# Second channel product of three of four batches by seven products of quarters in place of eight, with new hand-written orders

## The chip, the cores and the metric

The kernel runs on one core of a Trainium2 chip. The metric is the device time of one execution in microseconds (us), from runs of the same program; the median counts. Beside it stands one execution taken by the hardware profiler, whose trace is what the readings below come from.

The engines are named as the profile names them: PE multiplies matrices, PEld is its loading of the stationary operand, DVE, ACT and POOL are the vector, scalar and general engines, SP issues stores and some loads.

## What is computed

Windowed attention with four sink tokens, then one block that mixes tokens and channels, for 4 batches of 768 tokens, 8 heads of 64 (512 channels).

```python
def _attn_ref(q, k, v, n_sink, window):
    ...
    scores = scale * np.matmul(q, k.transpose(0, 1, 3, 2))
    ...
    scores = np.where(is_sink | in_window, scores, -1000000000.0)
    ...
    return np.matmul(a, v).astype(np.float32)

def _moe_ref(x, w_tok1, w_tok2, w_ch1, w_ch2):
    xt = x.transpose(0, 2, 1)
    h = np.maximum(xt @ w_tok1, 0.0) @ w_tok2
    u = x + h.transpose(0, 2, 1)
    h2 = np.maximum(u @ w_ch1, 0.0) @ w_ch2
    return (u + h2).astype(np.float32)
```

`w_tok1` is 768x256, `w_tok2` 256x768, `w_ch1` 512x1536, `w_ch2` 1536x512. The change is in the last product, `relu(u @ w_ch1) @ w_ch2`: 768x1536 by 1536x512 for each batch.

## The kernel before

**Stages.** Attention is done by pairs of heads, 4 pairs to a batch. Transposed scores come from PE, ACT takes the exponential from PSUM into `pT` (L620), DVE cuts the band out with a minimum against a mask (L638; L631 is the same on POOL), PE multiplies by the values, DVE normalises into `x_sb` (L744, L747). Token mixing follows for each half of the channels: `mix_h`, `mix_u` (its addition is L854) and a transposition into `uT`. Then channel mixing in `mix_channels`: `v1` multiplies `uT` by `w_ch1` in 24 units of four matmuls of 384 columns, each evicted with the relu into `v1T` by ACT (L159) or DVE (L161); and the second channel product, which `whole` makes for one tile of 128 tokens as 12 matmuls of 512 columns (four units of three), with one DVE addition of `u` on eviction (L1140) and one store of 256 KB (L1146). In the last batch the sixth tile is cut by `columns` into pieces of 256, 128 and 128 columns, with additions at L1175 and stores at L1180. All matmuls go through the helper `mm` (L146); in that second product `v1T` is the stationary operand, loaded for each matmul, and `w_ch2` moves.

**One buffer.** `v1T` is one tile for all batches. So each eviction into it waits for the last units of the second product of the batch before (`done["out", b - 1]`). PE's own matmuls of the next batch may run ahead into PSUM, which has eight banks, and be held there.

**Seven products.** The code for another way stood in the kernel, unused: `BY_SEVEN` (L64) lists the batches that take it, and was empty. In it a batch's `v1T` counts as quarters A11 to A22 (half of the tokens by half of the features) and `w_ch2` as quarters B11 to B22 (half of the features by half of the channels). `add_up` makes four sums of quarters of `v1T` on DVE or POOL, in two chunks each, `weight_sums` four of `w_ch2` once, `products` the seven products and what is added to the output.

**Order.** Nothing runs in an order found on the chip. `ORDERED` (L47) is the order of PE's units, one letter a stream: t, m, s, o, h, g the first batch's attention and token mixing; a, b, e, f, k those of the later ones (b and a scores and values of the attention, k token mixing); c the units of `v1`, 24 to a batch; x, and in the new version y, those of the second channel product. `LOADED` (L60) is the order of the loads on POOL's queue: v, q, k of a pair, t and c, d the quarters of the token and channel weights (d0 to d3 are `w_ch2`). The work of the other engines is put in between by `Plan`, which gives every operation a cost, a set of operations it waits for and an engine that is free first, and so fixes each engine's queue when the program is built. On the chip, each queue then runs strictly in that order. The costs in the diff are costs for this plan; they add no instruction by themselves.

Of the kernel before, what the change touches and what calls it, by code (L numbers as in the profile page):

```python
# [16 lines left out]
def kernel(  # L17
# [14 lines left out]
    B, H, S, D = q.shape  # L32
    P = 128
    NT = S // P
    DM = H * D
# [6 lines left out]
    HS = S // 2  # L42
# [2 lines left out]


    ORDERED = (  # L47
# [9 lines left out]
    )  # L57
    ORDER = (1, 2, 7, 6, 4, 5, 3)
    NQ = 6
    LOADED = (  # L60
        "v1 t0 v2 q4 v3 t1 k4 q5 c2 k5 c0 c1 k6 v4 q6 k7 v6 c3 v5 d3 q7 d2 d1 q8 q9 d0 k8 v7 q11 v8 k9 k10 v9 q15 "
        "k12 k11 q10 v10 q12 v14 k13 k14 v15 q13 v11 q14 k15 v13 v12"
    )
    BY_SEVEN = ()  # L64
    BY_DMA = 12
    U_BY_DMA = 2
    MASKED_BY_PE = [(p, g) for p in range(NHP) for g in range(NT // 2) if (p, g) != (NHP - 1, 0)]
# [98 lines left out]
    done = {}  # L166
# [802 lines left out]
    def mix_channels(b):  # L969
        units = []  # L970

        def v1(ft, half):
            def run():
                ps_v1 = tiles["ps_v1", b, ft, half] = bank("mx", HS)
                for ct in range(NC):
                    mm(
                        ps_v1.rearrange("f (t p) -> f t p", p=P), w_ch1[:, ct, ts(ft, P)], uT_half(b, ct, half),
                        start=(ct == 0), stop=(ct == NC - 1),
                    )

            def evict(e):
                if ("v1", b) not in tiles:
                    tiles["v1", b] = v1_pool.tile([P, NF, S], BF16, name="v1T")
                relu(e, tiles["v1", b][:, ft, ts(half, HS)], tiles["ps_v1", b, ft, half])

            op = Op(
                {"ACT": 490.0, "DVE": 550.0}, evict,
                done["out", b - 1] if b else [],
            )
            op.urgent = 1  # L990
            done["v1", b, ft, half] = op
            return unit(664, run, done["uT", b, half] + [done["ch1", ft * NW // NF]], {"mx": [[op]]}, [op])

        NH = NF // 2
        KC = NH // 2
        C2 = DM // 2

        def block(i, j, k0, n):
            return tiles["v1", b][:, j * NH + k0:j * NH + k0 + n, ts(i, HS)]

        def add_up(c):

            k0 = c * KC

            def part(n):
                if ("s", b) not in tiles:
                    tiles["s", b] = s_pool.tile([P, 3, NH, HS], BF16, name="v1_sums")
                return tiles["s", b][:, n, k0:k0 + KC]

            def op(name, out, in0, in1, how, deps):  # L1010
                def run(e):
                    in_order({"DVE": nc.vector, "POOL": nc.gpsimd}[e].tensor_tensor(
                        out=out(), in0=in0(), in1=in1(), op=how,
                    ))

                done[name, b, c] = Op({"DVE": 85.0 + 0.53 * KC * HS, "POOL": 150.0 + 2.2 * KC * HS}, run, deps)
                return done[name, b, c]

            a11, a12, a21, a22 = (lambda i=i, j=j: block(i, j, k0, KC) for i in range(2) for j in range(2))
            v = {(i, j): [done["v1", b, j * NH + k0 + n, i] for n in range(KC)] for i in range(2) for j in range(2)}  # L1020
            before = done["out", b - 1] if b else []
            s1 = op("S1", lambda: part(0), a21, a22, ALU.add, v[1, 0] + v[1, 1] + before)
            s3 = op("S3", a21, a11, a21, ALU.subtract, v[0, 0] + [s1])
            s2 = op("S2", lambda: part(1), lambda: part(0), a11, ALU.subtract, v[0, 0] + [s1])
            s4 = op("S4", lambda: part(2), a12, lambda: part(1), ALU.subtract, v[0, 1] + [s2])
            return [s1, s3, s2, s4]
# [164 lines left out]
        for c in range(2):  # L1191
            for half in range(2):
                units += [v1(j * NH + c * KC + n, half) for j in range(2) for n in range(KC)]
            if b in BY_SEVEN:
                units[-1].then += add_up(c)
        if b not in BY_SEVEN:
            last = b == B - 1
# [29 lines left out]
    def queue(key, op):  # L1227
        done[key] = op
        plan.pending.append(op)
# [26 lines left out]
    def weight_sums(c):  # L1256
        h, k = NF // 2, NF // NW
        b11, b12, b21, b22 = (
            w_ch2[:, j * h + c * k:j * h + (c + 1) * k, ts(g, DM // 2)] for j in range(2) for g in range(2)
        )  # L1260
        t1, t2, t3, t4 = (lambda n=n: sums_tile(n)[:, c * k:(c + 1) * k] for n in range(4))
        loaded = [done["ch2", c], done["ch2", 2 + c]]
        for name, out, in0, in1, of in (
            ("T1", t1, b12, lambda: b11, ()), ("T2", t2, b22, t1, ("T1",)),
            ("T3", t3, b22, lambda: b12, ()), ("T4", t4, b21, t2, ("T2",)),
        ):
            def run(e, out=out, in0=in0, in1=in1):
                in_order({"DVE": nc.vector, "POOL": nc.gpsimd}[e].tensor_tensor(
                    out=out(), in0=in0, in1=in1(), op=ALU.subtract,
                ))  # L1270

            queue((name, c), Op({"DVE": 85.0 + 0.53 * k * DM // 2}, run, loaded + [done[n, c] for n in of]))

    def sums_tile(n):
        while len(w_sums) <= n:
            t = raw_pool.tile([P, 2, NT * D], FP32, name="q_f")
            t = t.rearrange("p h x -> p (h x)").bitcast(BF16)
            w_sums.append(t.rearrange("p (k c) -> p k c", c=DM // 2))
        return w_sums[n]

    for c in range(2 if BY_SEVEN else 0):
        weight_sums(c)
# [18 lines left out]
    for word in ORDERED.split():  # L1301
        name, numbers = word[0], word[1:]
# [38 lines left out]
```

## Time and profile before

| | us |
|---|---|
| median of 3 runs | 205.5 |
| lowest and highest of them | 204.61, 205.73 |
| the profiled execution: its own time | 205.19 |
| the profiled execution: its span, first to last instruction | 203.5 |

The granted clock of PE was 1.0 over that execution. A line of a group reads: line of the kernel, engine, operation, output and inputs, shape, count, then busy time in us and the mean of one in ns, then the idle time of the engine just before them with what ended it. A line of the timeline reads: start and length in us, engine, line, operation, and in brackets the idle time before it. Matmuls overlap in the pipeline of PE, so the mean of one is its passage, not the pace; the pace is read from two starts.

### The profile page before, as it was taken

The numbers are of one execution on the slowest core, as the hardware profiler recorded it, in microseconds if no ns is written. First come the engines' busy times: TensorE is split into PE (matmuls) and PEld (weight loads), VectorE is DVE, ScalarE is ACT, GpSimd is POOL, SyncE is SP. The second block draws the span as 40 slices with busy tenths as digits, with TensorE's granted clock in tenths as the row PEclk, the third lists the DMA queues.
The fourth block names the chain that finished last, engine by engine and source line by source line (L and its number), as shares of the span: only waits on it lengthen the run. The fifth ranks groups of instructions, "written<-read, shape, count | busy, mean of one in ns | idle before, by whom it ended". The sixth has DMA issues, their size and how long they took to land.

```text
span 203.5 us, 5060 instructions
## 1 busy us (share of the span) xinstructions
PE 194.3 (95%) x2095; PEld 116.1 (57%) x2117; DVE 104.4 (51%) x237; ACT 111.1 (55%) x196; POOL 73.0 (36%) x108
## 2 busy tenths in 40 slices
PE   6789999999999999999999999999999999999993
PEld 2346886566565665566665454566765454664453
DVE  4787759667566777774557585722221223001221
ACT  4898789878835566677667234464562002773000
POOL 6199985976969800779110100200000000000000
PEclk9999999999999999999999999999999999999999
DMA  6999999999999994999976422210320113100223
GB/s 195 254 279 166 176 191 170 171 184 187 173 155 163 160 138 60 150 163 142 158 77 128 139 82 81 81 52 3 77 53 35 71 54 127 52 3 0 103 103 103
DMA packets 86151, 24.71 MB, mean 121 GB/s; under 512 B 76145, under 2 KB 83185, under 8 KB 86129
## 3 DMA queue, kind: packets, MB, share of 16 engines
q0 software_dynamic: 67232, 11.80, 73.9%
q1 hardware_dynamic: 18896, 12.60, 23.2%
q8 instruction: 16, 0.26, 0.6%
q14 instruction: 7, 0.05, 0.1%
HBM read 26.75 MB, written 6.29 MB: 162 GB/s over the span
## 4 chain that ended last, share of the span: by engine, by line
PE 80%; DMA 11%; POOL 5%; issue 1%; DVE 1%; SPq 0%; POOLq 0%
PE ps L146 77%; DMA w_ch<-in_moe_w_ch_dram 8%; DMA v_sink_f<-in_v_dram 3%; POOL v_aug L139 2%; POOL q_bf L131 1%; PE ps L549 1%; PE ps L149 1%; POOL w_tok L164 1%; PE ps L531 0%; PE ps L519 0%; SPq L225 0%; POOL q_bf L155 0%; POOL w_ch L164 0%; POOL v_sink L155 0%; DVE v_sink_f L221 0%
## 5 line engine op out<-in xcount | busy, mean ns | idle before, releaser
L146 PE MATMUL ps<-uT,w_ch 128*128 128x384 bf16 x384 | 68.0, 326 | 0.0
L146 PE MATMUL ps<-w_ch,v1T 128*128 128x512 bf16 (+2 forms) x293 | 65.7, 362 | 1.8 <-issue 0.6
L159 ACT ACTIVATE v1T<-ps 128x384 bf16<-128x384 f32 x82 | 39.9, 492 | 36.7 <-PE ps L146 34.5
L620 ACT ACTIVATE pT<-ps 128x1024 bf16<-128x1024 f32 (+1 forms) x48 | 44.3, 951 | 14.7 <-PE ps L146 14.5
L146 PEld LDWEIGHTS <-w_ch 128*128 128x128 bf16 x384 | 36.4, 98 | 23.9 <-issue 0.4
L146 PEld LDWEIGHTS <-v1T 128*128 128x128 bf16 x312 | 28.4, 98 | 27.5 <-issue 0.8
L1140 DVE TENSOR_TENSOR o_sb<-ps,u_sb 128x512 f32<-128x512 f32 x23 | 15.8, 686 | 39.9 <-PE ps L146 24.1
L146 PEld LDWEIGHTS <-w_tok 128*128 128x128 bf16 x192 | 18.3, 98 | 5.5
L139 POOL DMA_DIRECT2D v_aug<-in_v_dram x16 | 16.5, 1030 | 12.9 <-issue 7.0
L131 POOL DMA_DIRECT2D q_bf<-in_q_dram x24 | 19.8, 831 | 1.7 <-DMA w_ch<-in_moe_w_ch_dram 1.1
L131 POOL DMA_DIRECT2D k_bf<-in_k_dram x24 | 19.8, 836 | 1.5 <-DMA w_ch<-in_moe_w_ch_dram 1.2
L854 DVE TENSOR_TENSOR u_sb<-ps,x_sb 128x512 bf16<-128x512 f32 x20 | 13.7, 689 | 11.6 <-PE ps L146 8.0
L638 DVE TENSOR_TENSOR pT<-pT,mask_main 128x1024 bf16<-128x1024 bf16 (+1 forms) x23 | 14.3, 624 | 9.3 <-ACT pT L620 9.2
L146 PEld LDWEIGHTS <-pT 128*128 128x128 bf16 x352 | 14.4, 98 | 3.7 <-issue 0.2
L146 PE MATMUL ps<-qT,kT 64*64 64x192 bf16 (+3 forms) x288 | 16.5, 252 | 0.0
L146 PE MATMUL ps<-v_aug,pT 128*128 128x65 bf16 x352 | 15.9, 194 | 0.0
L146 PE MATMUL ps<-h1T,w_tok 128*128 128x256 bf16 x96 | 14.4, 273 | 0.1
L747 DVE TENSOR_TENSOR x_sb<-ps,recip 128x384 bf16<-128x384 f32 x24 | 12.9, 548 | 0.3
L146 PE MATMUL ps<-x_sb,w_tok 128*128 128x256 bf16 x96 | 12.0, 273 | 0.0
L146 PEld LDWEIGHTS <-kT 64*64 64x64 bf16 (+1 forms) x288 | 6.4, 101 | 7.9 <-issue 6.3
L161 DVE TENSOR_SCALAR v1T<-ps 128x384 bf16<-128x384 f32 x14 | 7.6, 552 | 6.1 <-PE ps L146 5.9
L638 DVE TENSOR_TENSOR pT<-pT,mask_first 128x1024 bf16<-128x1024 bf16 x13 | 8.9, 683 | 1.8 <-ACT pT L620 1.8
(69 smaller groups left out, 136.7 us busy)
## 6 DMA issues: line engine op xcount, KB each, us to landing
out_dram<-o_sb SPq DMA_DIRECT2D x23, 256.0 KB, 2.0
v_aug<-in_v_dram POOLq DMA_DIRECT2D x16, 192.0 KB, 6.7
w_ch<-in_moe_w_ch_dram POOLq DMA_DIRECT2D x8, 384.0 KB, 8.5
q_bf<-in_q_dram POOLq DMA_DIRECT2D x24, 96.0 KB, 6.1
k_bf<-in_k_dram POOLq DMA_DIRECT2D x24, 96.0 KB, 5.9
q_f<-in_q_dram SPq DMA_DIRECT2D x4, 384.0 KB, 5.8
k_f<-in_k_dram SPq DMA_DIRECT2D x4, 384.0 KB, 6.2
w_tok<-in_moe_w_tok_dram POOLq DMA_DIRECT2D x2, 384.0 KB, 6.5
```

What stands on the lines that cost most here:

```text
L131: in_order(nc.gpsimd.dma_start(out=out[:, h], in_=rows[:, h]))
L139: in_order(nc.gpsimd.dma_start(out=v_aug.rearrange("p i t d -> p (i t) d")[:, :, 0:D], in_=v[b].rearrange("h s d -> (h s) d")[2 * hp * S:2 ...
L146: in_order(nc.tensor.matmul(*args, skip_group_check=True, **kwargs))
L149: in_order(nc.tensor.transpose(out, in_, ident))
L159: in_order(nc.scalar.activation(out, in_, AF.Relu))
L161: in_order(nc.vector.tensor_scalar_max(out=out, in0=in_, scalar1=0.0))
L164: return in_order(nc.gpsimd.dma_start(out=out, in_=in_))
L620: in_order(nc.scalar.activation(part(tiles["pT", p][:, :, ds(2 * g, 2)]), of_keys(tiles["ps_s", p, g])[:, :, 0:width(g)], AF.Exp, scale=scale,
L638: in_order(nc.vector.tensor_tensor(out=pt, in0=pt, in1=m, op=ALU.min))
L747: in_order(nc.vector.tensor_tensor(out=x_sb[b][:, :, ds((2 * hp + i) * D, D)], in0=tiles["ps_o", p, i][:, :, 0:D], in1=tiles["recip", p, i ...
L854: in_order(nc.vector.tensor_tensor(out=u_part(b, g, s0, n), in0=tiles["ps_u", b, g, s0], in1=x_sb[b][:, s0:s0 + n, c0:c0 + cn], op=ALU.add,))
L1140: in_order(nc.vector.tensor_tensor(out=o_sb.rearrange("p (g c) -> p g c", g=2), in1=u_rows(b, st), in0=tiles["ps_out", b, st].rearrange("p ...
```

## The change

`BY_SEVEN` becomes batches 1 to 3. For these the second channel product is made by seven products of quarters. Batch 0 keeps `whole`; `columns` is no longer used. For each such batch `mix_channels` returns two streams: x, the seven products for token tiles 0 and 1 of each half (n = 2, two units of six matmuls to a product, 14 units), and y, for tile 2 of each half (n = 1, one unit of six, 7 units). Every matmul has 256 columns. `ORDER` gives the order of products: 1, 2, 7, 6, 4, 5, 3. `ORDERED` and `LOADED` are written anew, and three costs of the plan are changed.

The parts of `products` that the prediction follows, unchanged, with the sums they use:

```python
s1 = op("S1", lambda: part(0), a21, a22, ALU.add, v[1, 0] + v[1, 1] + before)
s3 = op("S3", a21, a11, a21, ALU.subtract, v[0, 0] + [s1])
s2 = op("S2", lambda: part(1), lambda: part(0), a11, ALU.subtract, v[0, 0] + [s1])
s4 = op("S4", lambda: part(2), a12, lambda: part(1), ALU.subtract, v[0, 1] + [s2])
...
TERMS = {
    1: ((0, 0), "B11"), 2: ((0, 1), "B21"), 3: ("S4", "B22"), 4: ((1, 1), "T4"),
    5: ("S1", "T1"), 6: ("S2", "T2"), 7: ("S3", "T3"),
}
...
a1 = evict("a1", (0, 0), lambda: u_block(0, 0))
a6 = evict("a6", (1, 0), lambda: u_block(1, 0))
c7 = evict("c7", (1, 1), lambda: u_block(1, 1))
a5 = evict("a5", (1, 1), lambda: sb(1, 1), [c7])
a3 = evict("a3", (0, 1), lambda: u_block(0, 1))
c4 = evict("c4", (1, 0), lambda: sb(1, 0), [a6])
b2 = evict("b2", (0, 0), lambda: sb(0, 0), [a1])
```

Products 1, 6, 5, 3 follow one another in one PSUM bank (a), 7 and 4 in another (c), 2 in a third (b). Each is evicted by one DVE addition, and the next product of its bank adds to what stands there, so it waits until that eviction has read the bank. Two stores leave for each stream: rows of the first half after a3 and b2, rows of the second after a5 and c4.

```diff
--- before.py
+++ after.py
@@ -45,23 +45,24 @@
 
 
     ORDERED = (
-        "t0-1 m0 s0 m1-2 t2 s1 t3 s2 m3 s3 o0 m4 t4 s4 m5 o1 t5 s5 o2 m6 t6 s6 m7 o3 s7 t7 m8 o4 s8-10 m9-10 g0 "
-        "s11 e0 s12 o5-6 g1 o7-8 g2-4 h0-1 g5-7 e1 h2-4 a0 h5-6 a1 e2 a2 h7 c0-6 a3 b0 a4 c7-11 b1 e3 a5 b2 "
-        "c12-13 b3 c14-15 a6 b4 a7 b5-6 c16-18 e4 a8 c19-20 k0 c21 a9 b7 a10 k1 c22 x0 c23 a11 b8 x1 k2 x2 b9-10 "
-        "x3 e5 b11-13 x4-6 e6 a12-13 x7-9 k3 x10 k4 x11-12 k5 b14 a14 f0 x13-14 k6 x15 k7 a15-16 b15-16 x16-17 f1 "
-        "e7 a17 x18-19 b17 x20-22 c24 a18 b18 e8 b19 x23 c25-27 b20 c28 a19-20 b21 c29-32 k8 a21 b22 a22 c33 b23 "
-        "c34-35 b24 c36-38 k9 c39-43 a23 b25 a24 c44-47 b26 k10 x24 b27 a25 b28 a26 x25-26 k11 x27 a27-28 k12 "
-        "x28-32 a29 b29 a30 x33 b30 x34 k13 x35 b31 k14 x36-37 a31-32 b32 x38 b33 x39-40 b34 x41-42 b35 a33-34 "
-        "x43-45 k15 b36 a35 b37-38 c48 x46-47 c49-52 b39 c53 b40 c54 k16 c55-56 b41 c57 x48 k17 c58 k18 c59 "
-        "k19-20 c60-62 k21-22 c63-71 x49-52 c72 x53-58 c73 x59-60 c74 x61-62 c75 k23 x63-71 c76-94 x72 c95 x73-94"
+        "t0-1 m0-1 s0 t2 m2 s1 t3 s2 m3 s3 m4-5 o0 t4 s4 t5 s5 o1-2 m6 t6 s6 o3 m7 t7 s7 m8 o4 s8-10 m9 g0 m10 "
+        "s11-12 g1 o5-8 g2-5 h0-1 g6 e0-1 h2-4 a0 h5-6 g7 h7 e2 a1 c0-4 b0 a2-3 c5-8 a4-5 b1-2 c9-12 b3 e3-4 b4-5 "
+        "c13-17 b6 c18 a6-7 c19-21 x0 c22 a8-9 b7 k0 c23 x1-2 a10 e5 b8-10 x3-4 k1 x5 a11-12 x6-7 a13 b11 k2 x8 "
+        "e6 a14 b12-13 x9-12 a15 b14 a16 k3-4 x13-14 e7 f0 a17 x15 k5 x16-18 k6-7 x19-21 b15 f1 e8 x22 b16 x23 "
+        "c24 b17 c25-27 a18 b18 a19 b19-20 c28-29 b21 a20-21 c30 k8 c31-32 a22 b22 a23 b23 c33-42 k9 b24 k10 "
+        "c43-44 a24-25 b25-27 k11 x24 a26 c45-47 x25 b28 a27-28 x26 y0 k12 a29 b29 x27 y1 b30 x28 k13 y2 x29-30 "
+        "b31 x31 y3 x32 k14 x33 y4 x34-35 a30 b32 a31 b33-34 x36 y5 a32 b35 a33 x37 c48 k15 c49 y6 c50-51 b36 "
+        "a34-35 c52 b37-38 c53 k16 c54 b39 c55 k17 c56-57 b40 k18 b41 c58 x38 k19 c59-61 k20 c62-63 k21 y7 k22 "
+        "c64-65 x39 c66-67 x40 c68 x41 c69-72 y8 c73 k23 x42 c74 x43 y9-10 x44-46 y11 x47-49 y12 c75 x50 c76 x51 "
+        "y13 c77-92 y14 c93-95 y15 x52-58 y16 x59-62 y17 x63 y18-19 x64-65 y20"
     )
     ORDER = (1, 2, 7, 6, 4, 5, 3)
     NQ = 6
     LOADED = (
-        "v1 t0 v2 q4 v3 t1 k4 q5 c2 k5 c0 c1 k6 v4 q6 k7 v6 c3 v5 d3 q7 d2 d1 q8 q9 d0 k8 v7 q11 v8 k9 k10 v9 q15 "
-        "k12 k11 q10 v10 q12 v14 k13 k14 v15 q13 v11 q14 k15 v13 v12"
+        "v1 t0 v3 v2 t1 q4 k4 c2 c0 k5 q5 q6 c1 v4 q7 c3 k6 v5 k7 d3 d2 k8 d0 q9 d1 v6 v8 q8 v7 k12 k9 q13 v11 "
+        "q11 q10 k10 k11 v13 q15 v10 q14 v9 v12 k13 q12 v14 v15 k15 k14"
     )
-    BY_SEVEN = ()
+    BY_SEVEN = range(1, B)
     BY_DMA = 12
     U_BY_DMA = 2
     MASKED_BY_PE = [(p, g) for p in range(NHP) for g in range(NT // 2) if (p, g) != (NHP - 1, 0)]
@@ -1013,7 +1014,7 @@
                         out=out(), in0=in0(), in1=in1(), op=how,
                     ))
 
-                done[name, b, c] = Op({"DVE": 85.0 + 0.53 * KC * HS, "POOL": 150.0 + 2.2 * KC * HS}, run, deps)
+                done[name, b, c] = Op({"DVE": (1012.0 if name == "S3" else 755.0), "POOL": 150.0 + 2.2 * KC * HS}, run, deps)
                 return done[name, b, c]
 
             a11, a12, a21, a22 = (lambda i=i, j=j: block(i, j, k0, KC) for i in range(2) for j in range(2))
@@ -1269,7 +1270,7 @@
                     out=out(), in0=in0, in1=in1(), op=ALU.subtract,
                 ))
 
-            queue((name, c), Op({"DVE": 85.0 + 0.53 * k * DM // 2}, run, loaded + [done[n, c] for n in of]))
+            queue((name, c), Op({"DVE": 150.0 + 0.53 * k * DM // 2}, run, loaded + [done[n, c] for n in of]))
 
     def sums_tile(n):
         while len(w_sums) <= n:
```

## The prediction

> **What bounds the kernel now.** I read the page's shares first, then what PE waited for, then the pace of its matmuls in the timeline.
>
> ```profile
> span 203.5 us, 5060 instructions
> PE 194.3 (95%) x2095; PEld 116.1 (57%) x2117; DVE 104.4 (51%) x237; ACT 111.1 (55%) x196; POOL 73.0 (36%) x108
> ...
> PE 80%; DMA 11%; POOL 5%; issue 1%; DVE 1%; SPq 0%; POOLq 0%
> ```
>
> PE is busy 95% of the span and is 80% of the chain that ended last. The list of PE's waits is short:
>
> ```profile
> PE ps L146 <- DVE ones L173: 1.5, 1, 1.5
> PE ps L531 <- DVE k_bf L155: 1.2, 3, 0.5
> PE ps L146 <- issue: 0.6, 4, 0.2
> PE ps L146 <- DMA w_ch<-in_moe_w_ch_dram: 0.4, 1, 0.4
> ```
>
> All of them but 0.6 us of issue and 0.4 us for a weight's landing lie in the first 16 us. From there PE is the bound, and work taken from PE shortens the end as long as nobody else becomes late. But a busy PE isn't proof of pace, so I read the pace from starts. Twelve matmuls of 256 columns, each with its own stationary operand, in token mixing:
>
> ```profile
> 143.57 1.47 PE L146 MATMUL ps<-x_sb,w_tok 128*128 128x256 bf16 x12
> 144.88 2.11 PE L146 MATMUL ps<-uT,w_ch 128*128 128x384 bf16 x12
> ```
>
> (144.88 - 143.57) / 12 = 0.109 us for one. The second channel product's own pace shows in the tail, where nothing else runs:
>
> ```profile
> 189.92 0.69 DVE L1140 TENSOR_TENSOR o_sb<-ps,u_sb 128x512 f32<-128x512 f32 x1 [1.90 <-PE ps L146]
> 192.51 0.69 DVE L1140 TENSOR_TENSOR o_sb<-ps,u_sb 128x512 f32<-128x512 f32 x1 [1.90 <-PE ps L146]
> ...
> 197.63 0.69 DVE L1140 TENSOR_TENSOR o_sb<-ps,u_sb 128x512 f32<-128x512 f32 x1 [1.90 <-PE ps L146]
> 198.94 0.42 DVE L1175 TENSOR_TENSOR o_sb<-ps,u_sb 128x256 f32<-128x256 f32 x1 [0.62 <-PE ps L146]
> 199.61 0.29 DVE L1175 TENSOR_TENSOR o_sb<-ps,u_sb 128x128 f32<-128x128 f32 x1 [0.24 <-PE ps L146]
> 200.28 0.29 DVE L1175 TENSOR_TENSOR o_sb<-ps,u_sb 128x128 f32<-128x128 f32 x1 [0.38 <-PE ps L146]
> ```
>
> A tile of twelve matmuls of 512 columns takes 192.51 - 189.92 = 2.59 us, 0.216 us each. Twelve of 256 columns take 198.94 - 197.63 = 1.31 us, again 0.109 each, now with v1T as stationary; twelve of 128 take 200.28 - 199.61 = 0.67 us, 0.056 each. So the time goes with the columns, and more loads of the stationary operand don't show:
>
> ```profile
> L146 PEld LDWEIGHTS <-v1T 128*128 128x128 bf16 x312 | 28.4, 98 | 27.5 <-issue 0.8
> ```
>
> a load lasts 98 ns, yet matmuls with a load each follow every 56 ns.
>
> **The change, part by part.**
>
> *Products.* Eight products of quarters are 72 matmuls of 512 columns in a batch: 6 x 2.59 = 15.54 us. The last batch has five such tiles, 12.95, and the pieces, 1.31 + 2 x 0.67: 15.60 us. Seven products are 7 x 18 = 126 matmuls of 256 columns at 0.109: 13.76 us (1.31 / 12 x 126). Gain 1.78 + 1.78 + 1.84 = **5.40 us** of PE time.
>
> The Trainium skill, "TensorE: Matmul & The Clock Gate", section "Back-to-back issue gap", has a rule against this: in a stream of pairs of load and matmul the spacing is set by both, about 81 ns at 128 columns and 131 ns at 512. A straight line between gives an estimate of 98 ns at 256, so 126 would take 12.3 us against 9.4 us for 72, a loss of 2.9 us a batch, and the time would be near 205.2 + 8.7 = 213.9. The trace doesn't agree: 216 ns at 512 and 56 ns at 128. I go by the trace, and keep what it would mean as a rival.
>
> *Sums of v1T.* New on DVE: eight operations of 128x1152 for each batch, 24 in all, both inputs in SBUF. Nearest rows, by shape:
>
> ```profile
> L638 DVE TENSOR_TENSOR pT<-pT,mask_main 128x1024 bf16<-128x1024 bf16 x12 | 8.2, 685 | 2.5 <-ACT pT L620 2.5
> L638 DVE TENSOR_TENSOR pT<-pT,mask_main 128x768 bf16<-128x768 bf16 x11 | 6.1, 557 | 6.8 <-ACT pT L620 6.7
> ```
>
> 128 ns for 256 columns more, so 0.75 us at 1152. The other bound is the pace of an addition from PSUM, 0.69 us at 512 and 0.42 at 256 columns: 0.27 per 256, 1.36 us at 1152. I take 0.75 for three of four; for S3, which overwrites its own input in rows with gaps, 1.0, between the two, since the mask also overwrites its input, without gaps. That's 2 x (3 x 0.75 + 1.0) = 6.5 us a batch (6.0 to 10.9).
>
> *Sums of w_ch2.* Eight operations of 128x768, once: 8 x 0.56 = 4.5 us (to 7.7 at the slower pace, 8 x 0.96).
>
> *Additions to the output.* Seven of 512 and seven of 256 columns take the place of six of 512: 7 x (0.69 + 0.42) - 6 x 0.69 = +3.6 us a batch on DVE.
>
> Together DVE gets 3 x 10.1 + 4.5 = 35 us more, on 104. What hides it is DVE's idle time, and the three stretches differ:
>
> ```profile
> 80.00:133.00 53.00, 52.42 (x579) 30.97 (x584) 34.99 (x74) 30.25 (x49) 16.88 (x29) 1.00 1.02 118
> 133.00:203.50 70.50, 66.98 (x425) 38.76 (x428) 15.09 (x27) 23.06 (x47) 0.00 (x0) 1.00 0.19 60
> 55.00:80.00 25.00, 24.05 (x393) 14.35 (x400) 17.42 (x38) 13.63 (x26) 14.19 (x20) 1.00 1.60 138
> ```
>
> (Columns: stretch, length, then PE, PEld, DVE, ACT, POOL.) Batches 2 and 3 fall after 133 us, where DVE is busy 15 of 70: 20 us more cost nothing there. Batch 1 falls into 80 to 133 with the attention of batches 2 and 3: 35.0 + 6.5 + 3.6 = 45.1 us of DVE work, or 49.6 with all sums of w_ch2, in 53 - 1.8 = 51.2 us. It fits, at 97% in the worst case; and evictions of v1T and copies of q and k that DVE does now can go to ACT, idle 23 us there. I count it as hidden, and price the other case as a rival.
>
> *New waits on PE.* A product on a sum waits for v1T's eviction and the chain S1, S3. Tightest is the last batch: between its last v1 unit (c95) and the second half of product 7 (x57) stand y15 and x52 to x56, 36 matmuls, 3.93 us. The chain: 0.16 until ACT starts, 0.49 for the eviction,
>
> ```profile
> 184.03 0.49 ACT L159 ACTIVATE v1T<-ps 128x384 bf16<-128x384 f32 x1 [0.16 <-PE ps L146]
> ```
>
> 0.75 + 1.0 for the sums, and 0.69 + 0.42 for two output additions queued on DVE between them: 3.5 us, so covered by 0.4. In batch 2 stand c72, y8, c73, k23, x42, c74 between: 3 x 0.65 (0.49 + 0.16 in that row, as ACT keeps step with PE) + 2 x 0.66 + 4 x 0.109 = 3.7 us against a like chain with k23's addition. A product that follows its bank's eviction needs about 0.16 + 0.69 = 0.85 us; the orders put at least two units of y (1.31 us) there at the end. If S3 or DVE's queue is late, product 7 waits, and behind it in PE's queue everything. Bounds: nothing, to one uncovered eviction (0.85) in each of three batches, 2.6. I take **+0.6**, near the low end as the covers exceed the chains.
>
> *The end.* The last addition grows from 128 to 256 columns, +0.13. The last store from 64 to 256 KB:
>
> ```profile
> out_dram<-o_sb SPq DMA_DIRECT2D x23, 256.0 KB, 2.0
> out_dram<-o_sb SPq DMA_DIRECT2D x1, 128.0 KB
> out_dram<-o_sb SPq DMA_DIRECT2D x2, 64.0 KB, 1.6
> ```
>
> +0.4, and up to 0.4 more where the 512 KB of x's last store are still on the way (1.07 us at the slope of these rows, less 0.66 head start). I take **+0.53**.
>
> *Moved steps.* In the first attention the masks m1 and m5 go ahead of other units, and e0 and e1, which turn q4 and k4, behind o8 and h1. In POOL's queue q4 goes from 4th to 6th place, behind v3 and t1, k6 from 13th to 17th, v6 from 17th to 26th, q7 from 21st to 15th, d0 from 26th to 23rd, d1 from 23rd to 25th. Each place is one or two issues:
>
> ```profile
> L131 POOL DMA_DIRECT2D q_bf<-in_q_dram x24 | 19.8, 831 | 1.7 <-DMA w_ch<-in_moe_w_ch_dram 1.1
> L139 POOL DMA_DIRECT2D v_aug<-in_v_dram x16 | 16.5, 1030 | 12.9 <-issue 7.0
> 55.37 0.81 PE L146 MATMUL ps<-w_ch,v1T 128*128 128x512 bf16 x2 [0.38 <-DMA w_ch<-in_moe_w_ch_dram]
> ```
>
> The one load that PE waits for later than 16 us is a w_ch quarter, 0.38 us, and d0 comes earlier. q4 leaves up to two issues (2.1 us) later, but PE asks for it later too. Between -0.4 (that wait goes) and +1.0 (one issue of a load uncovered); I take 0, the nearest row being a wait of 0.38 in the whole trace, of either sign.
>
> *Sum* against the profiled execution: 205.19 - 5.40 + 0.6 + 0.53 = **200.9 us**; that execution stands 0.3 below the median of the runs, and I leave it so. Low 205.19 - 5.40 + 0.53 - 0.4 = 199.9; high 205.19 - 5.40 + 2.6 + 0.93 = 203.3.
>
> **The rivals.**
>
> *The batch boundary eats part.* v1T is one buffer, so c72 to c76 stay in five PSUM banks until x51 and y13 have run, while x and y hold two more for their a and one or two for c. Before, PE ran through that boundary and ACT and DVE emptied the banks after it:
>
> ```profile
> 171.68 1.02 DVE L161 TENSOR_SCALAR v1T<-ps 128x384 bf16<-128x384 f32 x2 [1.90 <-PE ps L146]
> 171.74 1.73 ACT L159 ACTIVATE v1T<-ps 128x384 bf16<-128x384 f32 x4 [17.50 <-PE ps L146]
> ```
>
> With eight banks taken, a unit waits for the last additions, 0.69 + 0.42, and one eviction, 0.49: 1.6 us at each of two boundaries, with 5.40 and 0.53 as above 200.3 + 3.2 = **203.5**. For it: the counts come to seven or eight banks. Against it: b's banks are free long before.
>
> *DVE becomes the bound, slower.* In the stretch of batch 1. If the sums run at the slower pace, it has 35.0 + 10.9 + 7.7 + 3.6 = 57.2 us to do in 51.2: 6.0 over, **206.3**. Or the sums are quick, but DVE's queue is as strictly in order as now and sits idle for the exponentials as it did:
>
> ```profile
> DVE pT L638 <- ACT pT L620: 7.2, 7, 3.2
> ```
>
> 35.0 + 7.2 + 14.6 = 56.8, 5.6 over, 205.9; both together about 213. It decides the sign from 5 us over. Against it: the mask, also two inputs from SBUF, has the quick pace; ACT has room; the sums of w_ch2 can go ahead of 80 us.
>
> *Loads of the stationary operand stick out.* Each of 54 loads more per batch costs its 98 ns: 3 x 5.3 = 15.9, **216**. Only the twelve by twelve of the tail speak to it, and against it.
>
> **How the numbers follow.** My forecast has 0.62, the boundary 0.19, DVE as the bound 0.13 (two thirds of it over 206.5), the loads 0.03; 0.03 stay for anything else. The predicted time is the forecast's, 200.9. From 199.8 to 204.4 lies the forecast's own range and the boundary's case with 0.9 us to spare; left out are the other rivals and a stray. What this measurement can tell from no change is about 0.5%, 1 us. Faster: 0.62 + 0.19 and 0.02 of a part of the DVE case, 0.83. The same, 204.5 to 206.5: 0.06. Slower: 0.11.
>
> **What would show it.** The products of x and y at a pace of 0.109 us, 13.8 us of PE for each batch; sums of 0.75 and 1.0 us; PE's waits on DVE sums and additions at 0.6 us in all; DVE below 95% between 80 and 131 us; about 0.5 us more between the last matmul and the end. Wrong it would be if PE's idle time after 16 us grew by over 2.6 us, or if matmuls of 256 columns kept a longer pace than those of the token mixing.

## The result and the profile after

| | before | changed |
|---|---|---|
| median, us | 205.54 (4 runs, 204.61 to 205.73) | 203.16 (4 runs, 202.71 to 204.03) |
| ratio to before, 95% interval | | 0.9898 (0.9853 to 0.9943) |
| profiled execution: time, span, us | 205.19, 203.5 | 203.24, 201.5 |

Faster by 1.0%, where 2.2% was forecast: the sign is right, the time lies in the range, the size is off by half. Taken again in a later series, the changed kernel gave 203.44 us (ratio 0.9914, 0.988 to 0.9948).

First the page of the changed kernel, its span and shares:

```profile
span 201.5 us, 5425 instructions
PE 193.1 (96%) x2255; PEld 130.6 (65%) x2255; DVE 135.7 (67%) x289; ACT 110.2 (55%) x196; POOL 85.0 (42%) x122
```

DVE rose by 31 us (35 were counted), and PE fell by 1.2 us only; but a busy PE is no pace. The lines of the helper `mm` moved by one, to L147. The pace, in the timeline, inside batch 2's products (start, length, engine, line, operation, count; `q_f` holds the sums of w_ch2):

```profile
162.50 2.13 PE L147 MATMUL ps<-q_f,v1T 128*128 128x256 bf16 x18
164.46 2.13 PE L147 MATMUL ps<-q_f,v_sums 128*128 128x256 bf16 x18
166.43 0.81 PE L147 MATMUL ps<-uT,w_ch 128*128 128x384 bf16 x4
```

18 matmuls in 1.96 and 1.97 us: 0.109 us each, as forecast. What PE waited for:

```profile
PE ps L147 <- DVE v1T L1013: 0.5, 1, 0.5
...
PE ps L550 <- DMA q_bf<-in_q_dram: 0.4, 1, 0.4
```

The two longest of the new ones. The first is in the last batch, at the second half of product 7:

```profile
184.27 2.36 POOL L1013 TENSOR_TENSOR v_sums<-v_sums,v1T 128x1152 bf16<-128x1152 bf16 x1 [48.89 <-DVE v_sums L1013]
184.43 2.81 DVE L1013 TENSOR_TENSOR v1T<-v1T 128x1152 bf16<-128x1152 bf16 x1
185.97 0.82 PE L147 MATMUL ps<-q_f,v1T 128*128 128x256 bf16 x6
187.30 0.83 PE L147 MATMUL ps<-q_f,v1T 128*128 128x256 bf16 x6 [0.51 <-DVE v1T L1013]
```

S3 took 2.81 us on DVE while POOL made S2 beside it. Six matmuls from 185.97 would have been through at 186.63; the next began at 187.30, 0.67 us later. And the end:

```profile
194.58 2.13 PE L147 MATMUL ps<-w_ch,v_sums 128*128 128x256 bf16 x18
196.09 1.08 DVE L1059 TENSOR_TENSOR o_sb<-ps,u_sb 128x512 f32<-128x512 f32 x2 [0.88 <-PE ps L147]
```

PE is done at 194.58 + 18 x 0.109 = 196.54; the second of these additions begins at 196.09 + 1.08 - 0.42 = 196.75. From there to the end of the span it's 4.75 us; before, from 200.28 to 203.5, it was 3.2: the end grew by 1.5 us, to the 0.1 us to which the spans are given. How long stores took from issue to landing, on the page after:

```profile
out_dram<-o_sb SPq DMA_DIRECT2D x12, 256.0 KB, 3.0
out_dram<-o_sb SPq DMA_DIRECT2D x6, 512.0 KB, 2.8
```

So the account of the profiled execution is: products -5.4, the wait on S3 +0.7, the end +1.5, in sum -3.2. The span fell by 2.0. **1.2 us** are left that none of these explains; the wait of 0.4 on q5's load is a first trace of them.

### The profile page after: what moved, and what is told of

Its sections match the earlier page's. It is cut to its first block, busy times and chain, and to the rows that moved or that the text cites. A ratio compares the mean times of both kernels' runs of the same rounds, so it can differ in the third digit from the quotient of the medians.

```text
span 201.5 us, 5425 instructions
## 1 busy us (share of the span) xinstructions
PE 193.1 (96%) x2255; PEld 130.6 (65%) x2255; DVE 135.7 (67%) x289; ACT 110.2 (55%) x196; POOL 85.0 (42%) x122
## 4 chain that ended last, share of the span: by engine, by line
PE 79%; DMA 10%; POOL 3%; DVE 3%; issue 1%; SPq 0%; ACT 0%; POOLq 0%
PE ps L147 77%; DMA w_tok<-in_moe_w_tok_dram 4%; DMA q_bf<-in_q_dram 4%; DMA v_sink_f<-in_v_dram 3%; PE ps L550 2%; POOL v_aug L140 1%; DVE v1T L1013 1%; DVE o_sb L1059 1%; PE ps L520 1%; SPq L226 0%; POOL k_bf L132 0%; POOL w_tok L165 0%; POOL q_bf L132 0%; POOL q_bf L156 0%; POOL v_sink L156 0%
## 5 line engine op out<-in xcount | busy, mean ns | idle before, releaser
L147 PE MATMUL ps<-uT,w_ch 128*128 128x384 bf16 x384 | 68.5, 326 | 0.0
L160 ACT ACTIVATE v1T<-ps 128x384 bf16<-128x384 f32 x80 | 39.1, 492 | 36.5 <-PE ps L147 36.0
L147 PEld LDWEIGHTS <-w_ch 128*128 128x128 bf16 x384 | 36.5, 98 | 22.0 <-issue 0.4
L147 PEld LDWEIGHTS <-v1T 128*128 128x128 bf16 x288 | 27.4, 98 | 10.6 <-DVE v1T L1013 0.8
L147 PE MATMUL ps<-w_ch,v1T 128*128 128x256 bf16 (+1 forms) x180 | 31.5, 315 | 0.0
L1013 POOL TENSOR_TENSOR v_sums<-v_sums,v1T 128x1152 bf16<-128x1152 bf16 x2 | 4.7, 2362 | 49.8 <-DVE v_sums L1013 49.8
L147 PEld LDWEIGHTS <-w_tok 128*128 128x128 bf16 x192 | 18.1, 98 | 4.3 <-issue 0.4
L1059 DVE TENSOR_TENSOR o_sb<-ps,u_sb 128x512 f32<-128x512 f32 (+1 forms) x24 | 12.9, 553 | 9.0 <-PE ps L147 7.8
L147 PEld LDWEIGHTS <-v_sums 128*128 128x128 bf16 x162 | 15.6, 98 | 2.3 <-issue 0.2
L632 POOL TENSOR_SCALAR_AFFINE_SELECT pT<-pT 128x256 bf16<-128x256 bf16 (+1 forms) x20 | 8.6, 463 | 19.3 <-ACT pT L621 16.8
L147 PE MATMUL ps<-qT,kT 64*64 64x192 bf16 (+3 forms) x288 | 16.6, 255 | 0.0
L147 PE MATMUL ps<-v_aug,pT 128*128 128x65 bf16 x352 | 15.3, 194 | 0.2 <-DMA v_aug<-in_v_dram 0.2
L147 PEld LDWEIGHTS <-pT 128*128 128x128 bf16 x352 | 13.8, 97 | 2.3 <-issue 0.4
L147 PE MATMUL ps<-h1T,w_tok 128*128 128x256 bf16 x96 | 14.4, 273 | 0.0
L147 PE MATMUL ps<-q_f,v1T 128*128 128x256 bf16 x108 | 13.8, 273 | 0.5 <-DVE v1T L1013 0.5
L1059 DVE TENSOR_TENSOR o_sb<-ps,o_sb 128x512 f32<-128x512 f32 (+1 forms) x18 | 9.9, 554 | 6.2 <-PE ps L147 6.1
L147 PE MATMUL ps<-q_f,v_sums 128*128 128x256 bf16 x108 | 13.4, 273 | 0.0
```

The lines of the kernel that those rows point to most:

```text
L147: in_order(nc.tensor.matmul(*args, skip_group_check=True, **kwargs))
L160: in_order(nc.scalar.activation(out, in_, AF.Relu))
L632: in_order(nc.gpsimd.affine_select(out=pt, in_=pt, compare_op=ALU.is_ge, fill=0.0, base=-n, pattern=[[0, nk], [1 - 2 * n, P]], channel_mul ...
L1059: in_order(nc.vector.tensor_tensor(out=sb(*out), in0=tiles["ps_out", b, t0, key[0]], in1=in1(), op=ALU.add,))
```

## The experiments

All changes are against the changed kernel, unless said otherwise. Ratios are to the kernel before, measured beside it.

| kernel | median, us | ratio (95% interval) |
|---|---|---|
| again | 203.44 | 0.9914 (0.988 to 0.9948) |
| dve_sums | 202.58 | 0.9879 (0.9839 to 0.9919) |
| tail_cols | 202.00 | 0.9846 (0.9805 to 0.9886) |
| both | 201.37 | 0.9806 (0.9783 to 0.9828) |
| last_eight | 202.38 | 0.9875 (0.9836 to 0.9913) |
| eight_dve | 202.39 | 0.9860 (0.9828 to 0.9891) |
| batch1_eight | 203.51 | 0.9938 (0.9915 to 0.996) |
| batch2_eight | 202.85 | 0.9912 (0.9885 to 0.994) |
| both_again | 201.16 | 0.9827 (0.9798 to 0.9855) |
| all_eight | 206.32 | 1.0077 (1.0047 to 1.0107) |
| both_third | 201.59 | 0.9825 (0.9789 to 0.9862) |
| q5_early | 201.26 | 0.9812 (0.9779 to 0.9846) |
| e2_later | 205.02 | 0.9986 (0.9968 to 1.0003) |
| start_old | 203.24 | 0.9915 (0.9886 to 0.9944) |
| old_head | 207.10 | 1.0111 (1.0076 to 1.0146) |
| new_head | 209.86 | 1.0234 (1.021 to 1.0257) |
| before_again | 205.63 | 1.0018 (1.0001 to 1.0035) |

### The sum on POOL

```diff
-                done[name, b, c] = Op({"DVE": (1012.0 if name == "S3" else 755.0), "POOL": 150.0 + 2.2 * KC * HS}, run, deps)
+                done[name, b, c] = Op({"DVE": 755.0}, run, deps)
```

> All sums of v1T on DVE, none on POOL (two were). Theory 1 (a sum on POOL slows the sum that runs on DVE beside it): S3 of the last batch falls from 2.81 to 0.76 us, PE's wait of 0.51 us before product 7 goes, and the time falls by 0.5 to 0.7 us to about 202.5. Rival (S3 is slow because it overwrites its own input): S3 stays above 1.0 us and the time stays at 203.2.

Measured 0.86 us below the changed kernel beside it, where 0.5 to 0.7 were expected. The edit also lowers S3's cost in the plan; the order of PE's and ACT's work stays the same. In the groups by shape, S3 (v1T<-v1T) of the changed kernel, then of this one:

```profile
L1013 DVE TENSOR_TENSOR v1T<-v1T 128x1152 bf16<-128x1152 bf16 x6 | 8.4, 1407 | 0.1
```

```profile
L1013 DVE TENSOR_TENSOR v1T<-v1T 128x1152 bf16<-128x1152 bf16 x6 | 4.5, 753 | 0.1
L1013 DVE TENSOR_TENSOR v_sums<-v_sums,v1T 128x1152 bf16<-128x1152 bf16 x6 | 4.5, 750 | 0.0
```

In place or not, 0.75 us. In the changed kernel's own trace, too, the four S3 that ran without a sum on POOL took 0.75 to 0.76 us, and the two beside one 2.61 and 2.81. Overwriting its own input costs S3 nothing; the company on POOL did, and PE's wait on S3 is gone.

### The last stores

```diff
+            by_columns = b == B - 1
+            s00, s01, s10, s11 = (store_columns(i, g) for i in range(2) for g in range(2))
+            for st, o in ((s00, b2), (s01, a3), (s10, c4), (s11, a5)):
+                st.deps.append(o)
...
-                3: product(3, "a", a3, a5, [st0]),
+                3: product(3, "a", a3, a5, [s01 if by_columns else st0]),
```

(s00 goes with product 2, s10 with 4, s11 with 5.)

> In the last batch each store is cut in two by columns, the half that is complete early leaves early: behind the last product only 256 KB of x and 128 KB of y are left in place of 512 and 256. Theory 1 (the last store waits behind the 512 KB ahead of it): from its issue to its landing 1.6 to 2.0 us in place of 2.96, the time falls by about 1.0 us to 202.2. Rival (a store's landing has a fixed length, and shorter rows are slower): from issue to landing 2.8 us or more, the time stays within 0.3 us of 203.2 or grows.

Measured 1.4 us below the changed kernel beside it. Its last two additions and the four small stores:

```profile
196.50 1.08 DVE L1059 TENSOR_TENSOR o_sb<-ps,u_sb 128x512 f32<-128x512 f32 x2 [0.89 <-PE ps L147]
```

```profile
out_dram<-o_sb SPq DMA_DIRECT2D x4, 128.0 KB, 2.0
```

```profile
span 200.8 us, 5424 instructions
```

From the last addition's start, 196.50 + 1.08 - 0.42 = 197.16, to the end it's 3.6 us in place of 4.75. So the landing isn't fixed. This edit halves the last store and the one ahead of it alike, and so doesn't tell the two apart. The trace of the changed kernel does; its twelve stores of this kind:

```profile
DMA to landing us min/median/max: 2.0/2.8/3.0
```

The shortest, 2.0 us, is one of 256 KB issued 2.7 us behind the store ahead of it. The last one, also 256 KB, is issued 0.48 us behind the 512 KB and lands 2.96 us after its issue: about 1 us for the bytes ahead.

> Sums of v1T on DVE alone and stores of the last batch by columns, together. If the two costs are separate, the gains add: 203.3 - 0.9 - 1.4 = 201.0 us, no wait on S3 and a landing of the last store within 2.0 us. If one covers the other: 202.0.

Both cures together: 201.37 us, 1.9 under 203.24 (start_old beside it, below, which is as fast as the changed kernel) and 2.1 under 203.44, of 2.3 for the sum. This is faster than either of the two kernels compared.

### What seven products give, batch by batch

The last batch by eight, first with the plan still free to put sums on POOL (last_eight), then with all of them on DVE (eight_dve):

```diff
-    BY_SEVEN = range(1, B)
+    BY_SEVEN = range(1, B - 1)
...
-        ... y13 c77-92 y14 c93-95 y15 x52-58 y16 x59-62 y17 x63 y18-19 x64-65 y20"
+        ... y13 c77-95 x52-74"
```

> Seven products in batches 1 and 2 alone, the last batch by eight as before, with its small last pieces. Theory 1: PE's gain of 1.84 us in the last batch is given back there by the wait on S3 (0.67) and the longer end (1.57), so the time falls by about 0.4 us against the changed kernel, to 202.8. Rival (the gain of the last batch is real and was lost elsewhere, in the start or in batch 1): the time grows by 1.2 us or more, to 204.4 or above.

202.38: taking the change out of the last batch made the kernel faster by 1.06 us, even more than expected. As the change was made, its third batch was a loss.

> Seven products in batches 1 and 2, the last batch by eight, sums on DVE alone. In the last batch seven products save 1.84 us of PE; if the wait on S3 and the long end were all that ate it, the kernel with both cures (201.4) is faster than this one by 1.2 to 1.8 us, so 202.6 to 203.2 here. If something else in the last batch eats the saving too, the two are within 0.4 us.

202.39, 1.0 us over the 201.37 of the kernel with both cures, which was measured on another chip (by the ratios 1.1): a little under the expected range. The rows say where PE stood. Last additions of eight_dve, then of the kernel with both cures:

```profile
197.83 0.29 DVE L1176 TENSOR_TENSOR o_sb<-ps,u_sb 128x128 f32<-128x128 f32 x1 [0.38 <-PE ps L147]
```

```profile
195.38 1.08 DVE L1059 TENSOR_TENSOR o_sb<-ps,u_sb 128x512 f32<-128x512 f32 x2 [0.89 <-PE ps L147]
```

The last addition starts at 197.83 and at 195.38 + 1.08 - 0.42 = 196.04: seven products end 1.79 us earlier (1.84 forecast), and 0.7 of it go to a still longer end.

Then batches 1 and 2, each by eight products in the kernel with both cures:

```diff
-    BY_SEVEN = range(1, B)
+    BY_SEVEN = (2, 3)
```

(or `(1, 3)`; the 21 units of x and y of that batch become 24 units of x in the same places.)

> The kernel of both cures, with batch 1 by eight products: its 21 units of x and y become 24 units of three matmuls of 512 columns in the same places, batches 2 and 3 stay by seven. If batch 1's gain of 1.78 us of PE arrives in full at the end: 201.4 + 1.8 = 203.2. If the 1 us that is still missing is lost in batch 1 (DVE at 9.8 of 10 us between 110 and 120): 202.2 or less.

> The same with batch 2 by eight products, batches 1 and 3 by seven. If batch 2's gain of 1.78 us arrives in full: 203.2. If the missing 1 us is lost at its boundaries: 202.2 or less. If both this and batch 1 give 1.8, the missing 1 us lies ahead of the products, in the first 97 us.

> The kernel of both cures again, beside the other two: 201.4 us, within 0.4.

203.51 and 202.85 against 201.16: by the medians batch 1 costs 2.35 us, batch 2 1.69. Not all of that is the products. Up to a batch's first unit of the second channel product the two kernels make the same units, and still they don't come there together. That unit of batch 1 in batch1_eight and in both_again:

```profile
106.17 0.81 PE L138 MATMUL ps<-w_ch,v1T 128*128 128x512 bf16 x3
105.66 0.82 PE L147 MATMUL ps<-w_ch,v1T 128*128 128x256 bf16 x6
```

and that of batch 2 in batch2_eight and in both_again:

```profile
140.33 0.81 PE L138 MATMUL ps<-w_ch,v1T 128*128 128x512 bf16 x3
140.94 0.82 PE L147 MATMUL ps<-w_ch,v1T 128*128 128x256 bf16 x6
```

The spans are 201.8, 200.4 and 199.4 us. batch1_eight is 0.5 us late before its batch begins and 2.4 at the end: 1.9 us for batch 1. batch2_eight is 0.6 us early and then 1.0 late: 1.6 us for batch 2. For the last batch the spans of eight_dve and of the cured kernel, 200.8 and 199.7, give 1.1 us, where 1.84 less the 0.7 of the longer end were due. So the products yield about what was forecast, in every batch, and what is missing lies outside them.

> The new orders of units and loads, with eight products in all batches: the units of x and y become units of three matmuls of 512 columns in the same places, or next after the last v1 unit of their batch; the end is that of the kernel before, and no sums are made. If the missing 1 us is the new order's, ahead of the products: 206.2 to 206.6, 1 us over the kernel before on the same chip. If the new order costs nothing: within 0.4 us of the kernel before.

> The kernel of both cures beside it: 201.2 to 201.4, and 5.0 us below the new order with eight products (5.4 of PE less 0.45 at the end).

The new orders with no product by seven: 206.32 us, **1.3 us slower than the kernel before** (ratio 1.0077, 1.0047 to 1.0107, which is 1.0 to 2.2 us), and 4.7 us above the cured kernel beside it. There 5.40 were due, less the 0.45 by which the cured end is still longer than that of before (3.82 us from PE's last matmul to the end of the span, against 3.37): 4.95. Its page and what PE waited for:

```profile
span 204.5 us, 5074 instructions
```

```profile
PE ps L541 <- DMA q_bf<-in_q_dram: 0.6, 1, 0.6
PE ps L523 <- DVE k_bf L147: 0.5, 2, 0.3
PE ps L138 <- issue: 0.3, 2, 0.2
```

The missing 1.2 us come with the new orders as a whole, also without a product by seven.

### Where the new orders lose it

> The changed kernel itself, taken again. Theory 1 (the start differs by execution): in the first profile PE ran at half pace until 10.6 us (512 columns in 427 ns) where the kernel before had left it at 6.1 us, with the same matmuls on PE up to there; in another execution the change to full pace comes at another time, and the times spread by about 1 us, 202.7 to 204.0. Rival (the new order of the first attention causes it): again half pace until about 10.6 us, and a spread no wider than 0.3 us.

> The kernel before, taken again for its start. If the time at which PE reaches full pace differs by execution, it may be at 6 or at 10 us here, and the idle time of PE before 20 us changes by 0.3 to 0.8 us with it; if the order fixes it, again 6.1 us.

The start does differ by execution, and in the kernel before as well. Four masks in its first profile and in its second:

```profile
7.11 0.93 PE L146 MATMUL ps<-mask_add,ident 128*128 128x512 bf16 x4
```

```profile
7.65 1.67 PE L146 MATMUL ps<-mask_add,ident 128*128 128x512 bf16 x4
...
9.44 0.38 PE L146 MATMUL ps<-qT,kT 64*128 64x256 bf16 x4
```

The second time PE runs at half pace until 9.3 us. Yet both spans are 203.5 us: the half pace cost nothing that reached the end. The same units of that kernel at 31 us, in the first profile and in the second:

```profile
30.86 0.36 PE L146 MATMUL ps<-qT,kT 64*64 64x192 bf16 x8
```

```profile
31.43 0.36 PE L146 MATMUL ps<-qT,kT 64*64 64x192 bf16 x8
```

The second execution is 0.57 us late there, and at 92.7 us only 0.03 (rows further down). In between, the first waits 0.38 us for a quarter of w_ch at 55.4 us, and the second doesn't. The changed kernel taken again left the half pace at 9.3 to 9.6 us, where its first profile had left it at 10.6; so theory 1 of the start holds, but as an explanation of the missing time it falls, since the slower start of before lost no time.

For the old order of units up to o0:

> The changed kernel with the old order of units up to o0 alone, the first 14 us; the loads stay as changed. If the new order of the start costs 0.5 us: 202.8 and less idle time on PE before 20 us. If not: 203.3, within 0.3.

203.24: nothing. For the old order and loads up to the first unit of v1 in the changed kernel (old_head, shown here), and the new ones in the kernel before (new_head):

```diff
-        "t0-1 m0-1 s0 t2 m2 s1 t3 s2 m3 s3 m4-5 o0 ...
+        "t0-1 m0 s0 m1-2 t2 s1 t3 s2 m3 s3 o0 m4 ...
...
-        "v1 t0 v3 v2 t1 q4 k4 c2 c0 k5 q5 q6 ...
+        "v1 t0 v2 q4 v3 t1 k4 q5 c2 k5 c0 c1 ...
```

> The changed kernel with the old order of units up to the first unit of v1 and the old order of loads. Theory 1: 203.2 us, within 0.4. Rival (the new order of the first attention or of the loads costs 1.2 us): 202.0 or less, full pace on PE from about 6 us.

> The kernel before with eight products, but with the new order of units up to the first unit of v1 and the new order of loads. Theory 1 (the start's extra 1.2 us in the profile isn't the order's): 205.5 us, within 0.4. Rival (the new order of the first attention or of the loads costs it): 206.5 or more, with half pace on PE until about 10 us.

Both mixtures are slower than both kernels, 207.10 and 209.86, and decide nothing: each brought a wait of its own, such as this one in old_head, for a later load,

```profile
PE ps L541 <- DMA q_bf<-in_q_dram: 2.7, 1, 2.7
```

since the rest of the order was made for other landings. They show how much such an order is worth, and that half of one can't be tried alone.

A wait before e2, for q5, shows in most profiles with the new loads, with 0.2 to 1.0 us (both_again and eight_dve don't have it). Two ways to take it away, moving PE's unit, or the load:

```diff
-        ... g7 h7 e2 a1 c0-4 b0 a2-3 ...
+        ... g7 h7 a1 c0-2 e2 c3-4 b0 a2-3 ...
```

> The changed kernel with one unit of PE moved: e2, which turns q5 and k5, goes behind three of the five v1 units that followed it, about 2 us later. Theory (q5's load, moved from 8th to 11th place, lands at 32.1 us and PE stands before e2 for 0.4 to 1.2 us): the wait on that load goes and the time falls by 0.4 to 1.0 us to about 202.7. Rival (the wait only moves, since the scores of that pair are next and late by as much): the time stays at 203.3, and PE waits for the copies of q5 or k5 instead.

The wait is gone, others have come (0.8 us on a load of v, 0.4 on an addition to the output), and the median rose to 205.02. Moving one unit also reordered the work of ACT, DVE and POOL behind it, and the profiled execution was the fastest of twelve (203.65), so what slowed the others isn't known.

```diff
-        "v1 t0 v3 v2 t1 q4 k4 c2 c0 k5 q5 q6 ...
+        "v1 t0 v3 v2 t1 q4 k4 k5 q5 c2 c0 q6 ...
```

> The kernel of the two cures (sums on DVE alone, last stores by columns), with q5 and k5 loaded ahead of the two first quarters of w_ch1 in place of behind them; PE's order stays but for the buffers' names. Theory (PE waits before e2 because q5's load came three places later): the wait of 0.6 us on that load goes, 200.7 us. Rival (the loads bound the first 65 us together, so the wait moves to w_ch1 or a later load): 201.4, with a wait on another load in its place.

201.26, no gain over 201.37. The wait before e2 is gone, and PE waits for a k later:

```profile
44.16 0.35 PE L550 MATMUL ps<-ident,k_bf 64*128 64x64 bf16 x12 [0.48 <-DMA k_bf<-in_k_dram]
```

The rival holds. Where the orders lose can be read at one place. Ahead of b22 in the old order and of a22 in the new one the kernels have made the same units, 1257 matmuls. The row that follows, in the kernel before, in its second profile, in the changed kernel and in all_eight:

```profile
92.71 0.28 PE L146 MATMUL ps<-v_sink,pT_sink 64*128 64x65 bf16 x8
92.74 0.28 PE L146 MATMUL ps<-v_sink,pT_sink 64*128 64x65 bf16 x8
93.68 0.36 PE L147 MATMUL ps<-qT,kT 64*64 64x192 bf16 x8
93.34 0.36 PE L138 MATMUL ps<-qT,kT 64*64 64x192 bf16 x8
```

The changed kernel is 1.0 us late there and all_eight 0.6, ahead of any product by seven. Counted by the loads of the stationary operand, all twelve profiles that keep both new orders up to this place are late against the first one of the kernel before, by 0.2 to 1.8 us and by 1.1 in the mean. On average 0.6 us of it arise between 31 and 37 us, where most of them wait before e2. So most of what is missing is lost in the first 93 us. Which of the moved loads and units cause it stays open, since curing the wait for q5 brought nothing.

## Why the prediction was wrong

**Right: the products.** 5.40 us of PE, at 0.109 us a matmul; by single batches 1.9, 1.6 and 1.1 us arrived, where 1.78, 1.78 and 1.1 were due, and over all_eight 4.7 of 4.95. The rule of the Trainium skill, "TensorE: Matmul & The Clock Gate", section "Back-to-back issue gap" (131 ns at 512 columns, 81 at 128), didn't hold here: the kernel before shows 216 and 56 ns, and 256 columns go at 109 ns in products whose every matmul loads its own stationary operand. The rival of loads that stick out is gone with it.

The forecast for the profiled execution was -5.4 + 0.6 + 0.53 = -4.3 us, and the span fell by 2.0. The missing 2.3 us are two terms of the sum.

**Wrong, the largest step: the moved steps.** They were taken at 0, between -0.4 and +1.0. The new orders alone cost 1.3 us (all_eight), and the changed kernel has lost 1.0 us by 93 us. The step failed twice: the prediction listed q4, k6, v6, q7, d0 and d1 but not q5, which moved from 8th to 11th place and is the load that the changed kernel's PE waits for longest (0.4 us, and 1.0 taken again; a v costs 0.2 and 0.3); and it argued from single loads, where the early loads and units are a chain in which a wait cured in one place comes back in another (q5_early, e2_later).

**Wrong: the end.** The forecast took +0.53 us, from medians of landings (1.6 and 2.0 us), and put at most 0.4 more on the 512 KB store ahead, of which it took nothing. It was 1.5. The median of 2.0 comes from stores that left 1.9 us or more apart, and that of 1.6 from small ones with at most 128 KB close ahead; here 256 KB were issued 0.48 us behind 512 KB, and landed 2.96 us later. Storing the finished columns early brought 1.2 of the 1.5 us back in the profile, 1.4 in the median.

**Right in size by luck, wrong in cause: the new waits.** +0.6 forecast, 0.67 found, in the last batch as named. But S3 isn't slow by overwriting its input, as the 1.0 us taken for it meant; it takes 0.75. The plan had put S2 on POOL beside it, which the prediction didn't look for, although POOL stood among the engines of that operation. Taking it away brought 0.86 us.

**The rivals.** The batch boundary cost nothing: PE has no wait there, and batch 2 gave 1.6 to 1.7 of 1.78. DVE wasn't the bound in batch 1's stretch, though nearly full in a part of it (9.8 of 10 us from 110 to 120). The windows of the changed kernel (stretch, length, PE, PEld, DVE, ACT, POOL):

```profile
80.00:131.20 51.20, 51.20 (x660) 36.07 (x658) 38.41 (x76) 29.22 (x48) 16.54 (x33) 1.00 0.79 104
```

38.4 of 51.2 us, 75%, and batch 1's products gave 1.9 us, no less than the 1.78 forecast.

With what was found, -5.4 + 1.5 + 0.7 + 1.0 = -2.2 with the loss read at 93 us, or -1.9 with the 1.3 of all_eight; the span fell by 2.0. That the time still lies in the range is luck as well: the range reaches as far as it does for up to 2.6 us of waits on sums and for the batch boundary. The waits came to 0.67 us, and that room took up what the end and the orders cost.

## What to carry to other kernels

Work saved on the bounding engine arrives in full only up to the last instruction: price the tail by what is queued ahead of the last store, and store finished columns as soon as they are final. When an edit comes with a new order, measure the new order without the edit; here it took back about a quarter of the products' gain. And where a planner may choose between two engines, look at what the two do to each other, not only at each one's own time.

## What was not expected of the hardware

- A DVE addition with both inputs in SBUF, 0.75 us alone, took 2.61 and 2.81 us while POOL ran a like one of 2.36 us. The Trainium skill, "GPSIMD Engine Reference", section "8. Key points", says that the two share SBUF interfaces and collide for DVE instructions with two SBUF inputs. The trace agrees; nothing would have been lost by making S2 on DVE.
- The time at which PE comes to full pace, 6.1 or 9.4 us, differs between two executions of one and the same kernel, with the granted clock on the profile's page at 9 tenths or more throughout. The Trainium skill, "TensorE: Matmul & The Clock Gate", section "What's actually happening", has it that the window of activity runs freely and the change varies by run. The trace agrees that it varies, though by 3.3 us, more than the 0.5 us either way that the section gives; and it adds that this didn't reach the end here, both spans being 203.5 us.
